# Attention and token mixer in one kernel: the attention-values product cut into 64x64 array tiles, its halves summed on VectorE

## The chip, the core and the metric

The kernel runs as one program on one core of a Trainium2 chip. The metric is the device time of one execution in microseconds (us). TensorE (PE in the profile) multiplies matrices into PSUM, which has eight banks; VectorE (DVE), ScalarE (ACT) and GpSimd (POOL) do the elementwise work; SyncE (SP) issues most of the DMA transfers. Every engine works through its own list in order.

## The reference

Causal softmax attention over 4 batches, 12 heads, 448 positions and 64 features per head, followed by a mixer over tokens and one over channels, all in float32 (x is the heads' outputs side by side, 4 x 448 x 768):

```python
scores = scale * np.matmul(q, k.transpose(0, 1, 3, 2))
scores = np.where(mask, -1000000000.0, scores)
...
attn = attn / (np.sum(attn, axis=-1, keepdims=True) + 1e-09)
attn_out = np.matmul(attn, v)
...
xt = x.transpose(0, 2, 1)
h = np.maximum(xt @ w_tok1, 0.0) @ w_tok2
u = x + h.transpose(0, 2, 1)
h2 = np.maximum(u @ w_ch1, 0.0) @ w_ch2
return u + h2
```

The causal mask means that of a head's 448x448 square only the lower triangle is computed.

## The kernel before

The work is cut into jobs. `plan.job(costs, fn, needs, holds, ...)` names the engines that may do a job, what it waits for and which buffers and PSUM banks it holds. Two tables of numbers in the code decide the rest: `PLACES` gives every job its place in one list (a smaller number goes first, if what it needs is ready by the costs that the jobs state), and `CHOICE` gives the engine (a, d, p, s for ScalarE, VectorE, GpSimd, SyncE) where several may do it. `Plan.emit` walks the list and writes the instructions of the five engines in that order. Where TensorE has nothing to do by these costs in the first 75 us of the program, `emit` writes a filler, a matmul on the mask tile whose result nobody reads (L865). A filler is an instruction like any other: it runs whether or not TensorE would have had to wait.

There are 24 pairs of heads (`g` from 0 to 23; the kernel's ranks are 2g). For each pair:

- `load_pair` and `load_rows` load Q, K and V. For pair 0 and from pair 6 on, Q and K come in blocks of 32x32 (L940, destinations kq, gh and gl), four transfers to a tensor, and VectorE turns them (`prep`, L988). For pairs 1 to 5 they come as rows (L892, L895) and TensorE turns them (L916, L910).
- `heads` makes the scores on TensorE in 64x64 tiles of the array (L1021), adds the mask and finds the maximum on VectorE (L1043), exponentiates on ScalarE (L1055), and takes the reciprocal of the sum on VectorE (L1077).
- `by_tensor` (pairs 0 to 9) divides and turns the probabilities on TensorE in 64x128 tiles (L1115); `by_dma` (pairs 10 to 23) turns them by DMA, with copies on VectorE and ScalarE (L640, L638). The result is the tile `pt`, with the key positions on the partitions.
- `values` multiplies V with `pt`. Its matmuls have 128 rows (keys) and 64 columns (a head's features), so two of them, one for each head, lie side by side in the array (L1245); two jobs `pv` per pair. The four ends of the triangle that are 64 keys wide, the tips, are a third job in 64x64 tiles (L1254). The left part of the 448 positions (192) goes to one PSUM bank (`low`), the right part (256) to another (`ps`). `evac` then copies the two parts to the tile `u` (helper `copy`: L632 on ScalarE, L634 on VectorE).
- After every second pair `xturn` turns `u` on TensorE in 64x128 tiles (L1291). Then follow `tokens` (L1350, L1383), and, batch by batch, the channel mixer (L1433; for the last two batches L1765, L1836, L1860). These have 128x128 tiles.

In the first 300 us the jobs of all these kinds are mixed on TensorE, so the shape of the tiles changes often. A matmul on float32 operands (L1021, L1245, L1254, L916) is two passes through the array, and shows as two records in the trace; one on fp32r, and a transpose, is one.

The two sets of pieces of the product are `PIECES` (pairs 0 to 9: eight pieces of 128 or 64 columns) and `SUMS` (pairs 10 to 23: four pieces of 256 or 128 columns).

Of the kernel before, what the change touches and what calls it, by code (L numbers as in the profile page):

```python
# [21 lines left out]
    "load_pair.blocks": {-2: (0, 1), 10: (129, 153), 12: (193, 224), 14: (242, 259), 16: (338, 293), 18: (405, 420),  # L22
        20: (522, 537), 22: (578, 591), 24: (670, 694), 26: (742, 758), 28: (831, 851), 30: (911, 927), 32: (996,
        1006), 34: (1056, 1070), 36: (1141, 1151), 38: (1205, 1220), 40: (1280, 1293), 42: (1333, 1348), 44: (1406,
        1426)},
    "load_pair.load": {0.5: (2,), 2.5: (3,), 4.5: (178,), 6.5: (209,), 8.5: (274,), 10.5: (312,), 12.5: (393,),
        14.5: (453,), 16.5: (490,), 18.5: (558,), 20.5: (615,), 22.5: (704,), 24.5: (773,), 26.5: (822,), 28.5:
        (902,), 30.5: (949,), 32.5: (1047,), 34.5: (1114,), 36.5: (1194,), 38.5: (1241,), 40.5: (1376,), 42.5:
        (1441,), 44.5: (1489,), 46.5: (1531,)},
    "load_pair.upper": {-0.2: (12,), 1.8: (15,), 3.8: (213,), 5.8: (245,), 7.8: (317,), 9.8: (380,), 11.8: (441,),  # L30
        13.8: (505,), 15.8: (519,), 17.8: (592,), 19.8: (651,), 21.8: (727,), 23.8: (821,), 25.8: (859,), 27.8:
        (938,), 29.8: (982,), 31.8: (1077,), 33.8: (1136,), 35.8: (1226,), 37.8: (1269,), 39.8: (1401,), 41.8:
        (1462,), 43.8: (1517,), 45.8: (1561,)},
# [500 lines left out]
def kernel(  # L534
# [74 lines left out]
    def act_ps(n):  # L609
        return 65.0 + 0.833 * n  # L610
# [1367 lines left out]
```

## Time and profile before

| | |
|---|---|
| median of 3 runs | 538.36 us (538.03 to 538.51) |
| the profiled execution | 538.04 us, of which the span from first to last instruction is 536.2 us |
| TensorE matmul busy | 529.8 us (99%) |
| VectorE, ScalarE, GpSimd busy | 426.4 (80%), 314.0 (59%), 164.2 us (31%) |
| granted TensorE clock | 1.00 over the span |

Busy times of matmuls overlap, since one starts while the one before still drains; how much time a matmul takes of the engine is read from the distance between two starts. The sums below are made against the profiled execution, 0.3 us under the median.

### The profile page before, as it was taken

The page shows a single profiled execution, that of the slowest core. Times are in us where ns is not written, and L with a number is a line of the kernel's source. Part 1 is how long each engine was busy: PE and PEld are TensorE (multiplying, and loading weights), DVE is VectorE, ACT ScalarE, POOL GpSimd, SP SyncE. Part 2 cuts the span into 40 slices and gives each one's busy share as a digit, 9 for nine tenths or more (in the row PEclk, how much of TensorE's full clock was granted, in tenths as well). Part 3 has the DMA queues.
Part 4 walks back from the last instruction along what each step waited for, and adds up shares of the span by engine and source line. Part 5 has one row for each costly group of instructions (what it writes and reads, how often), then busy time and mean ns, then how long its engine had stood idle before and what let it go on. Part 6 is the DMA issues. An engine that isn't in the chain of part 4 may idle for free.

```text
span 536.2 us, 12037 instructions
## 1 busy us (share of the span) xinstructions
PE 529.8 (99%) x4391; PEld 460.6 (86%) x4391; DVE 426.4 (80%) x1030; ACT 314.0 (59%) x768; POOL 164.2 (31%) x220
## 2 busy tenths in 40 slices
PE   8999999999999999999999999999999999999997
PEld 4778888888888888888898899999999999999996
DVE  5998899989797999888896679677877848485665
ACT  4998898899888787789784561243232313131300
POOL 2565745444252232332452132140010012321200
PEclk9999999999999999999999999999999999999999
DMA  9966677979999998999969327648213030212147
GB/s 194 198 116 144 152 214 160 215 153 233 207 178 200 225 190 193 205 196 229 210 163 198 115 92 205 131 119 162 88 32 116 7 91 23 87 32 88 31 75 131
DMA packets 221546, 77.72 MB, mean 145 GB/s; under 512 B 195760, under 2 KB 210992, under 8 KB 221488
## 3 DMA queue, kind: packets, MB, share of 16 engines
q1 hardware_dynamic: 207984, 74.90, 63.1%
q10 hardware_dynamic: 13504, 2.07, 2.1%
q8 instruction: 34, 0.56, 0.5%
q14 instruction: 24, 0.20, 0.2%
HBM read 49.15 MB, written 14.94 MB: 120 GB/s over the span
## 4 chain that ended last, share of the span: by engine, by line
PE 94%; SPq 2%; DVE 2%; ACT 1%; DMA 1%; issue 0%; POOL 0%; DVEq 0%; POOLq 0%
PE ps L1433 33%; PE ps L1860 16%; PE ps L1765 12%; PE ps L1021 6%; PE ps L1245 6%; PE ps L1383 6%; PE ps L1350 6%; PE ps L1836 3%; PE ps L1254 1%; PE ps L1115 1%; PE ps L1291 1%; SPq L940 1%; PE ps L865 1%; ACT prob L1055 1%; DMA gh<-in_k_dram 1%; PE ps L910 0%
## 5 line engine op out<-in xcount | busy, mean ns | idle before, releaser
L1500 DVE TENSOR_TENSOR u<-ps,u 128x448 f32<-128x448 f32 x118 | 72.5, 619 | 34.2 <-PE ps L1860 28.0
L1055 ACT ACTIVATE prob<-prob,stat 128x192 f32<-128x192 f32 (+6 forms) x168 | 83.7, 501 | 14.4 <-DVE stat L1043 14.1
L643 POOL TENSOR_TENSOR wl<-wf,wh 128x768 fp32r<-128x768 f32 x26 | 49.5, 1904 | 94.4 <-ACT wh L632 59.4
L1043 DVE CUSTOM_DVE_ANT_0 prob<-ps,mask 128x128 f32<-128x128 f32 (+6 forms) x168 | 63.3, 415 | 7.3 <-PE ps L1021 6.9
L634 POOL TENSOR_SCALAR prob<-prob,stat 128x64 f32<-128x64 f32 (+6 forms) x80 | 43.8, 559 | 55.4 <-DVE stat L1077 42.9
L1433 PE MATMUL ps<-uh,wh 128*128 128x448 f32 x144 | 53.7, 373 | 0.0
L1433 PE MATMUL ps<-gh,wh 128*128 128x448 f32 x144 | 52.9, 367 | 0.0
L1433 PE MATMUL ps<-gh,wl 128*128 128x448 f32 x144 | 52.7, 366 | 0.0
L1433 PE MATMUL ps<-gl,wh 128*128 128x448 f32 x144 | 52.7, 366 | 0.0
L1433 PE MATMUL ps<-uh,wl 128*128 128x448 f32 x144 | 52.7, 366 | 0.0
L1433 PE MATMUL ps<-ul,wh 128*128 128x448 f32 x144 | 52.7, 366 | 0.0
L632 ACT ACTIVATE wh<-wf 128x768 fp32r<-128x768 f32 x27 | 22.5, 846 | 51.2 <-PE ps L1860 25.8
L1021 PE MATMUL ps<-kq,kq 64*64 64x64 f32 (+5 forms) x768 | 45.4, 356 | 0.0
L1021 PEld LDWEIGHTS ps<-kq,kq 64*64 64x64 f32 x768 | 26.6, 133 | 15.5 <-issue 9.6
L1245 PE MATMUL ps<-pt,vraw 128*64 128x128 f32 (+2 forms) x544 | 37.3, 284 | 0.0
L1245 PEld LDWEIGHTS ps<-pt,vraw 128*64 128x64 f32 x544 | 28.2, 137 | 9.8 <-issue 2.1
L1795 DVE TENSOR_TENSOR kq<-kq,ps 128x448 f32<-128x448 f32 x35 | 21.2, 619 | 14.8 <-PE ps L1765 14.2
L1055 ACT ACTIVATION_READ_ACCUMULATOR prob<-prob,stat 128x1 f32 x168 | 32.1, 191 | 0.0
L638 ACT COPY pt<-pt 128x384 uint16<-128x384 uint16 (+3 forms) x41 | 31.6, 830 | 0.8 <-DMA pt<-prob 0.8
L1860 PE MATMUL ps<-u,wh 128*128 128x448 f32 (+1 forms) x110 | 31.0, 363 | 0.0
L1433 PEld LDWEIGHTS ps<-uh,wh 128*128 128x128 f32 x144 | 27.0, 188 | 2.8 <-issue 0.2
L1433 PEld LDWEIGHTS ps<-gl,wh 128*128 128x128 f32 x144 | 27.1, 188 | 2.5 <-DVE gl L1468 0.2
(222 smaller groups left out, 1403.2 us busy)
## 6 DMA issues: line engine op xcount, KB each, us to landing
wraw<-in_moe_w_ch_dram SPq DMA_DIRECT2D x24, 768.0 KB, 5.4
wf<-scratch SPq DMA_DIRECT2D x30, 384.0 KB, 3.1
scratch<-wf SPq DMA_DIRECT2D x24, 384.0 KB, 4.8
vraw<-in_v_dram SPq DMA_DIRECT2D x44, 96.0 KB, 3.4
kq<-in_k_dram SPq DMA_DIRECT2D x60, 56.0 KB, 3.7
kq<-in_q_dram SPq DMA_DIRECT2D x56, 56.0 KB, 2.4
out_dram<-h1l SPq DMA_DIRECT2D x24, 56.0 KB, 2.7
out_dram<-h1h SPq DMA_DIRECT2D x24, 56.0 KB, 2.2
```

The lines of the kernel that those rows point to most:

```text
L634: eng[e].tensor_scalar(dst, src, scale, 0.0, op0=ALU.mult, op1=ALU.add)
L643: eng[e].tensor_tensor(dst, a, b, op=ALU.subtract)
L1021: nc.tensor.matmul(scores[n].tile[lanes, to:at], lhsT=qe.tile[LANES[j], c * QC:(c + 1) * QC], rhs=ke.tile[LANES[j], slice(*keys)], start=T ...
L1043: nc.vector.tensor_tensor_reduce(out=part(c, r), in0=ps.tile[:, at:at + wide(c)], in1=mask[:, S - QC:S + P] if c == 2 else mask[:, S - wid ...
L1055: nc.scalar.activation(part(c, r), part(c, r), AF.Exp, bias=stat.tile[:, 0, AT[c]:AT[c] + 1], scale=-1.0, accum_out=stat.tile[:, 1, AT[c]: ...
L1245: nc.tensor.matmul(to, lhsT=s.tile[:, kb, j], rhs=rhs, start=(n in first_of), stop=False)
L1350: nc.tensor.matmul(ps.tile[:, :PART], lhsT=w[:, c, m * P:(m + 1) * P], rhs=x.tile[:, c, :], start=(n == 0), stop=(n == len(work) - 1),)
L1383: nc.tensor.matmul(ps.tile[:, :S], lhsT=h.tile[:, m, o * P:(o + 1) * P], rhs=w[:, m, :], start=(n == 0), stop=(n == 3 * NM - 1),)
L1433: nc.tensor.matmul(ps.tile[:, :S], lhsT=x.tile[:, at_:at_ + P], rhs=y, start=(n == 0 and i == 0), stop=(n + 1 == w[2] and i == 2),)
L1500: eng[e].tensor_tensor(u, ps.tile[:, :S], u, op=ALU.add)
L1765: nc.tensor.matmul(ps.tile[:, :S], lhsT=l()[:, t * P:(t + 1) * P], rhs=r, start=(t == 0 and n == 0), stop=(t == half - 1 and n == 2),)
L1860: nc.tensor.matmul(ps.tile[:, cols], lhsT=l.tile[:, t * P:(t + 1) * P], rhs=r.tile[:, cols], start=(n == 0), stop=(n == 3 * len(fs) - 1),)
```

## The change

The matmuls of the values product are split once more: the 128 keys of a piece become two halves of 64, so that each piece is four matmuls in 64x64 tiles instead of two in 128x64 tiles. The two halves can't be added in the array any longer: half 0 goes to the bank `ps`, half 1 to the bank `low`, each over all positions (half 0 has nothing in the first 64). The tips, which were 64x64 before, are written behind the second part in the same job. On the way out, `nought` copies all of `low` to `u` (ScalarE or VectorE), and `evac` adds 384 columns of `ps` on VectorE.

```diff
-        def chunks(n, j):
+        def chunks(n, j, half):
 
             if flat_:
-                which, kb, c, step, nq, o, stride = PIECES[n]
-                out = banks[which].tile[LANES[j]].rearrange("p (c q) -> p c q", q=QC)[:, c:c + step * (nq - 1) + 1:step]
-                rhs = pt.tile[:, 1 - j if c in OVER else j, o:o + stride * (nq - 1) + 1:stride]
+                _, kb, c, step, nq, o, stride = PIECES[n]
+                out = banks[half].tile[LANES[j]].rearrange("p (c q) -> p c q", q=QC)[:, c:c + step * (nq - 1) + 1:step]
+                rhs = pt.tile[LANES[half], 1 - j if c in OVER else j, o:o + stride * (nq - 1) + 1:stride]
...
                 for n in part:
+                    for half in range(2):
+                        for j in range(2):
+                            kb, to, rhs = chunks(n, j, half)
+                            nc.tensor.matmul(to, lhsT=s.tile[LANES[half], kb, j], rhs=rhs, start=n == 0, stop=False)
+                for half, kb, o, c in ENDS if part[0] else ():
                     for j in range(2):
-                        kb, to, rhs = chunks(n, j)
-                        nc.tensor.matmul(to, lhsT=s.tile[:, kb, j], rhs=rhs, start=(n in first_of), stop=False)
+                        nc.tensor.matmul(
+                            banks[half].tile[LANES[j], c * QC:(c + 1) * QC],
+                            lhsT=(ends if half else s).tile[LANES[half], kb, j], rhs=tip(o, c, j, half),
+                            start=False, stop=(o == 9),
+                        )
 
             prev = plan.job(
-                {"pe": 660.0 if part[0] else 718.0}, pv, js + pdone + [prev], [ps, low, s, ends, pt, u], rank, tiled=1
+                {"pe": 930.0 if part[0] else 705.0}, pv, js + pdone + [prev], [ps, low, s, ends, pt, u], rank, tiled=2
             )
...
-        prev = plan.job({"pe": 282.0}, tips, [prev], [ps, low, s, ends, pt, u], rank, tiled=2)
-
-        def evac(e):
+        def nought(e):
             if t == 0:
                 make(u, [P, NT, S], F32)
-            copy(e, u.tile[:, t, 3 * QC:], ps.tile[:, 3 * QC:S])
-            copy(e, u.tile[:, t, :3 * QC], low.tile[:, :3 * QC])
+            copy(e, u.tile[:, t], low.tile[:, :S])
+
+        def evac(e):
+            nc.vector.tensor_tensor(u.tile[:, t, QC:], ps.tile[:, QC:S], u.tile[:, t, QC:], op=ALU.add)
 
         first = [u_ready[b, 0]] if t else []
-        u_ready[b, t] = plan.job(
-            {"act": act_ps(S) + 65.0, "dve": dve1(S) + 70.0}, evac, [prev] + first, [ps, low, u], rank
-        )
+        c = plan.job({"act": act_ps(S), "dve": dve1(S)}, nought, [prev] + first, [low, u], rank)
+        u_ready[b, t] = plan.job({"dve": dve1(S - QC)}, evac, [prev, c], [ps, u], rank)
```

Both tables are new from end to end, so every engine's order changes, and which engine does what. A line of `CHOICE`:

```diff
-    "by_tensor.evac": {0: "dada", 2: "ddda", 4: "aaad", 6: "aada", 8: "adaa", 10: "aada", 12: "dada", 14: "ddaa",
+    "by_tensor.evac": {0: "daaa", 2: "dddd", 4: "adad", 6: "ddaa", 8: "aaaa", 10: "adda", 12: "daad", 14: "adaa",
```

Counted over TensorE's whole list, two neighbouring matmuls have tiles of different shape in 134 places before and in 120 after. Taking 128x128 as one group: it is left 37 times and entered 37 times before, 44 and 44 after; changes among the smaller shapes are 60 before and 32 after. Fillers are 27 before and 33 after, 16 and 13 of them ahead of the first scores. On VectorE the 24 adds are new, with five copies of 448 columns for two pairs of 192 and 256; ScalarE has 19 copies of 448 columns for 22 pairs of 192 and 256.

The first place is TensorE's list at the last values product (pair 23; matmuls of L1433, the channel mixer, stand ahead of it in both). Before:

```order
L1433 MATMUL ps_4606<-uh_2154,wl_4506 128x448
L1245 MATMUL ps_4648<-pt_4590,vraw_91 64x256 x2
L1245 MATMUL ps_4649<-pt_4590,vraw_91 64x128 x2
L1245 MATMUL ps_4648<-pt_4590,vraw_91 64x256 x2
L1245 MATMUL ps_4648<-pt_4590,vraw_91 64x128 x2
L1254 MATMUL ps_4648<-pt_4590,vraw_91 64x64 x2
L1254 MATMUL ps_4649<-pt_4590,vend_92 64x64 x2
L1254 MATMUL ps_4648<-pt_4590,vraw_91 64x64 x2
L1254 MATMUL ps_4649<-pt_4590,vend_92 64x64 x2
L1433 MATMUL ps_4672<-uh_1176,wh_4586 128x448
```

The same product after, from its second row on (L1246 are the pieces, L1249 the tips; ps_4829 is the bank of half 0, ps_4830 that of half 1):

```order
L1246 MATMUL ps_4830<-pt_4775,vraw_91 64x256 x2
L1246 MATMUL ps_4829<-pt_4775,vraw_91 64x128 x2
L1246 MATMUL ps_4830<-pt_4775,vraw_91 64x128 x2
L1246 MATMUL ps_4829<-pt_4775,vraw_91 64x256 x2
L1246 MATMUL ps_4830<-pt_4775,vraw_91 64x256 x2
L1246 MATMUL ps_4829<-pt_4775,vraw_91 64x128 x2
L1246 MATMUL ps_4830<-pt_4775,vraw_91 64x128 x2
L1249 MATMUL ps_4829<-pt_4775,vraw_91 64x64 x2
L1249 MATMUL ps_4830<-pt_4775,vend_92 64x64 x2
L1249 MATMUL ps_4829<-pt_4775,vraw_91 64x64 x2
L1249 MATMUL ps_4830<-pt_4775,vend_92 64x64 x2
L1348 MATMUL ps_4866<-xh_4792,w1hi 128x256
```

Eight rows of 128x64 tiles became sixteen matmuls of 64x64 tiles, of the same shape as the tips behind them; 22 matmuls of the token mixer (L1348) now stand between this product and the turn of `u` that waits for it, where six of the channel mixer stood.

The second place is the way out of the same product. Before, on ScalarE (u_3778 is the tile `u` of the last batch):

```order
L632 ACTIVATE prob_0_4657<-kq_4644 128x448
L632 ACTIVATE u_3778<-ps_4648 128x256
L632 ACTIVATE u_3778<-ps_4649 128x192
L632 ACTIVATE wh_4687<-wf_4642 128x768
L632 ACTIVATE xh_4717<-ps_4691 128x2x4x64
```

After, on VectorE (here both the copy and the add; in 19 pairs the copy is ScalarE's):

```order
L1466 SCALAR_TENSOR_TENSOR gl_4860<-ps_4794,gh_4841 128x448
L634 TENSOR_SCALAR u_3965<-ps_4830 128x448
L1265 TENSOR_TENSOR u_3965<-ps_4829,u_3965 128x384
L1361 SCALAR_TENSOR_TENSOR h1l_4897<-ps_4866,h1h_4895 128x256
L1361 SCALAR_TENSOR_TENSOR h1l_4897<-ps_4883,h1h_4895 128x256
```

Two copies on ScalarE became a copy and, behind it, an add on VectorE.

The third place is VectorE's list where it turns K of pair 8 (gh_786 before, gh_860 after; the load of that K is the fifth of the block loads L940 behind pair 0's on SyncE before and the sixth after). L1077 is a reciprocal that the division (L634) of the same probabilities waits for, L1363 (L1361 after) belongs to the token mixer. Before:

```order
L1077 RECIPROCAL stat_716<-stat_716 128x4
L988 STREAM_TRANSPOSE kq_915<-gh_786 128x448
L1363 SCALAR_TENSOR_TENSOR h1l_932<-ps_829,h1h_894 128x256
L634 TENSOR_SCALAR pt_939<-ps_900 128x448
L699 SCALAR_TENSOR_TENSOR wf_762<-wl_490,wf_762 128x224
L634 TENSOR_SCALAR prob_0_86<-prob_0_86,stat_716 128x320
```

After:

```order
L1265 TENSOR_TENSOR u_495<-ps_901,u_495 128x384
L988 STREAM_TRANSPOSE kq_1028<-gl_497 128x448
L1361 SCALAR_TENSOR_TENSOR h1l_1050<-ps_988,h1h_1024 128x256
L988 STREAM_TRANSPOSE kq_1056<-gh_860 128x448
L1361 SCALAR_TENSOR_TENSOR h1l_1050<-ps_1008,h1h_1024 128x256
L1077 RECIPROCAL stat_899<-stat_899 128x3
```

K of pair 8 moved ten rows back in VectorE's list (from row 138 to row 148), behind one add of the values product, and the division that stood four rows behind it no longer does. SyncE's list changes too: K of pair 1 as rows (uh, L892) is now the very first transfer, where it was the sixth row.

## Rows read from the trace of the kernel before

**Rows 1.** Page, span and busy time of each engine.

```profile
span 536.2 us, 12037 instructions
PE 529.8 (99%) x4391; PEld 460.6 (86%) x4391; DVE 426.4 (80%) x1030; ACT 314.0 (59%) x768; POOL 164.2 (31%) x220
```

**Rows 2.** Page, chain that ended last, by engine.

```profile
PE 94%; SPq 2%; DVE 2%; ACT 1%; DMA 1%; issue 0%; POOL 0%; DVEq 0%; POOLq 0%
```

**Rows 3.** Waits of PE over the span: total us, times, longest.

```profile
PE ps L865 <- POOL mask L650: 1.5, 1, 1.5
PE ps L916 <- DMA uh<-in_k_dram: 0.7, 1, 0.7
PE ps L1115 <- DVE stat L1043: 0.4, 1, 0.4
PE ps L1893 <- DVE u L1887: 0.3, 1, 0.3
```

**Rows 4.** Timeline of PE, last values product: start, length, instruction.

```profile
297.03 0.36 PE L1433 MATMUL ps<-ul,wh 128*128 128x448 f32 x1
297.23 0.36 PE L1433 MATMUL ps<-uh,wl 128*128 128x448 f32 x1
297.52 1.52 PE L1245 MATMUL ps<-pt,vraw 128*64 128x256 f32 x16
298.97 0.27 PE L1254 MATMUL ps<-pt,vraw 64*64 64x64 f32 x2
298.98 0.27 PE L1254 MATMUL ps<-pt,vend 64*64 64x64 f32 x2
299.08 0.22 PE L1254 MATMUL ps<-pt,vraw 64*64 64x64 f32 x2
...
299.13 0.23 PE L1254 MATMUL ps<-pt,vraw 64*64 64x64 f32 x2
...
299.19 0.23 PE L1254 MATMUL ps<-pt,vraw 64*64 64x64 f32 x2
...
299.36 0.48 PE L1433 MATMUL ps<-uh,wh 128*128 128x448 f32 x1
299.68 0.37 PE L1433 MATMUL ps<-ul,wh 128*128 128x448 f32 x1
```

**Rows 5.** Windows of L1021, four 64x64 scores of 256 or 320 columns start.

```profile
151.06:151.28 0.22, 0.21 (x4) 0.16 (x8) 1.00 0.60 104
151.28:151.49 0.21, 0.21 (x8) 0.13 (x1) 1.00 0.80 126
```

**Rows 6.** Timeline of PE, first 47 us, fillers and waits.

```profile
8.44 0.99 PE L916 MATMUL ps<-ident,ul 112*64 112x112 f32 x16
9.36 0.82 PE L865 MATMUL ps<-mask 128*128 128x512 bf16 x3
10.87 0.99 PE L916 MATMUL ps<-ident,uh 112*64 112x112 f32 x16 [0.68 <-DMA uh<-in_k_dram]
...
17.48 0.38 PE L865 MATMUL ps<-mask 128*128 128x512 bf16 x1
...
45.15 0.27 PE L1115 MATMUL ps<-ident,prob 64*128 64x64 f32 x1
45.83 0.65 PE L1115 MATMUL ps<-ident,prob 64*128 64x64 f32 x13 [0.41 <-DVE stat L1043]
```

**Rows 7.** Timeline of DVE, 40 to 45 us.

```profile
41.34 0.18 DVE L1077 RECIPROCAL stat<-stat 128x4 f32<-128x4 f32 x1
42.70 0.65 DVE L988 STREAM_TRANSPOSE kq<-gh 128x448 f32<-128x448 f32 x1 [1.18 <-DMA gh<-in_k_dram]
```

**Rows 8.** Timeline of SP, 30 to 43 us.

```profile
33.86 1.55 SPq L953 DMA_DIRECT2D vraw<-in_v_dram  x1
35.45 2.15 SPq L940 DMA_DIRECT2D gl<-in_q_dram  x4
37.65 2.04 SPq L940 DMA_DIRECT2D gh<-in_k_dram  x4
```

**Rows 9.** Windows, all engines, 50 to 300 us: PE, PEld, DVE, ACT, POOL.

```profile
50.00:300.00 250.00, 250.00 (x2486) 213.10 (x2486) 219.50 (x604) 207.87 (x528) 97.81 (x128) 1.00 0.91 192
```

**Rows 10.** Groups by form, VectorE, ScalarE and fillers: busy us, mean ns.

```profile
L1043 DVE CUSTOM_DVE_ANT_0 prob<-ps,mask 128x384 f32<-128x384 f32 x24 | 13.1, 547 | 0.0
L634 DVE TENSOR_SCALAR pt<-ps 128x448 f32<-128x448 f32 x16 | 9.7, 614 | 0.4 <-PE ps L1115 0.3
L632 ACT ACTIVATE pt<-ps 128x448 f32<-128x448 f32 x24 | 12.5, 533 | 0.0
L632 ACT ACTIVATE u<-ps 128x256 f32<-128x256 f32 x22 | 8.3, 378 | 12.6 <-PE ps L1254 12.4
L632 ACT ACTIVATE u<-ps 128x192 f32<-128x192 f32 x22 | 7.1, 324 | 0.0
L865 PE MATMUL ps<-mask 128*128 128x512 bf16 x27 | 8.7, 449 | 1.5 <-POOL mask L650 1.5
```

**Rows 11.** Timeline of PE, a product's tips to the turn of u.

```profile
150.78 0.27 PE L1254 MATMUL ps<-pt,vraw 64*64 64x64 f32 x2
...
151.01 0.22 PE L1254 MATMUL ps<-pt,vraw 64*64 64x64 f32 x2
...
151.98 0.71 PE L1291 MATMUL ps<-ident,u 64*128 64x64 f32 x16
```

More of the change, by code (lines that the diff above doesn't have):

```diff
@@ new lines @@
+    "channels.down": {28.5: (699,), 28.75: (735,), 29: (743,), 29.25: (761,), 29.5: (806,), 29.75: (781,), 36:
[6 rows of a table added]
+    "add.plus": {-6: (718, 756, 758, 775, 820, 790, 1090, 1073, 1080, 1055, 1127, 1121, 1180, 1153, 1214, 1221,
[6 rows of a table added]
+    "store.turn": {-5: (1752, 1768, 1785, 1786, 1798, 1807, 1843, 1837, 1861, 1856, 1876, 1870, 2236, 2237, 2242,
+        2243, 2245, 2251, 2253, 2257, 2262, 2266)},
+    "store.send": {-5: (1754, 1772, 1787, 1794, 1801, 1809, 1847, 1840, 1864, 1858, 1878, 1873, 2238, 2241, 2247,
+        2246, 2252, 2254, 2261, 2258, 2265, 2267)},
@@ new lines @@
+    "combined.sum_.do": {-4.94: (1886, 1888, 1889, 1892), -4.93: (1957, 1960, 1964, 1967), -4.92: (2018, 2019, 2022,
+        2024), -4.91: (2086, 2088, 2089, 2096), -4.9: (2143, 2146, 2151, 2156)},
+    "group.product.do": {55.44: (1880,), 55.71: (1885,), 55.98: (1908,), 56.25: (1905,), 56.52: (1932,), 56.79:
[5 rows of a table added]
+    "group.first.do": {-6: (1887, 1950, 2021, 2084, 2159)},
+    "group.plus.do": {-6: (1913, 1918, 1920, 1938, 1939, 1931, 1940, 1995, 1996, 1999, 2002, 2005, 2006, 2009, 2059,
+        2061, 2067, 2069, 2073, 2072, 2076, 2129, 2131, 2130, 2142, 2144, 2140, 2148, 2198, 2203, 2199, 2204, 2207,
+        2225, 2211)},
@@ L1226, in chunks @@
             view = pt.tile.rearrange("p o (j q) -> p o j q", j=2)
-            return kb, banks[c == 1].tile[LANES[j], c * QC:(c + nq) * QC], view[:, o, 1 - j if c in MIXED else j]
+            out = banks[half].tile[LANES[j], c * QC:(c + nq) * QC]
+            return kb, out, view[LANES[half], o, 1 - j if c in MIXED else j]
         def tip(o, c, j, half):
@@ L1249, in values @@
             )
-        def tips(e):
-            for half, kb, o, c in ENDS:
-                for j in range(2):
-                    nc.tensor.matmul(
-                        banks[half].tile[LANES[j], c * QC:(c + 1) * QC],
-                        lhsT=(ends if half else s).tile[LANES[half], kb, j], rhs=tip(o, c, j, half),
-                        start=False, stop=(o == 9),
-                    )
-        prev = plan.job({"pe": 282.0}, tips, [prev], [ps, low, s, ends, pt, u], rank, tiled=2)
```

297 lines of the change are left out of this document (139 added, 158 removed), and 198 rows, old and new, of tables (CHOICE, PLACES).

## The prediction

> **What bounds the kernel now.** I read the busy shares first: matmuls cover 529.8 us of a span of 536.2 [rows 1], and the chain that ended last lies on TensorE for 94% [rows 2]. Busy alone proves little, since matmuls overlap. So I looked at TensorE's waits: four places, 2.9 us in all [rows 3], of which 1.5 us is the start of the program. Between 50 and 300 us TensorE has no idle time at all, while VectorE is busy 219.5 and ScalarE 207.9 us of the 250 [rows 9]. The kernel is therefore as long as TensorE's list plus small waits in the first 50 us, and only what shortens the list, or those waits, shortens the kernel. VectorE, with 30.5 us free of 250, is the next engine that could bind.
>
> What TensorE's list costs beyond its columns is seen in one values product [rows 4]. The channel matmuls of 448 columns start 0.20 us apart. From the last of them to the first 128x64 matmul it is 0.29, so leaving the 128x128 shape costs 0.09. The tips' rounds start 0.06 us apart, but the first of them lasts 0.11, so the first round in a new shape costs 0.05. From the product's first start to the tips' it is 1.45 us. The product is 1536 columns of rounds (256, 256, 128, 128 twice, two passes included): 24 steps of 64 columns, at the tips' 0.055 a step 1.32 us. The rest, 0.13, is the first round's 0.05 and a drain of 0.08 before the tips' shape. On the way back, the last round to the first channel matmul takes 0.17 for 0.06, and that matmul 0.32 for 0.20. So a change of shape costs 0.14 us on leaving 128x128, 0.23 on coming back, and 0.13 among the small shapes (0.15 if the 256-column rounds are a little quicker per column than the tips').
>
> **The change, part by part.**
>
> Columns: nothing. The product has the same rounds after as before; only each holds four 64x64 tiles in place of two of 128x64. Would four run beside each other? The tips do it before: in the steps of 0.055 us four matmuls of 64 columns start, two to each bank, in the layout that the pieces have after [rows 4]. And four scores of 256 and 320 columns start together, with no other start for 0.22 us [rows 5], which is four steps of 0.055. So I cost the columns at zero; the bound is one of the rivals.
>
> TensorE: Matmul & The Clock Gate in the Trainium skill (section "Wait — 56ns, not 53.3ns?") says that two matmul starts never come closer than about 25 ns, however small they are. By that rule a round of four would take at least 100 ns, and the 64-column rounds would lose 42 ns each. Rows 4 speak against it: four starts fit into 55 ns here, so the rows' figure stands.
>
> Changes of shape: before 37 x 0.14 + 37 x 0.23 + 60 x 0.13 = 21.5 us, after 44 x 0.14 + 44 x 0.23 + 32 x 0.13 = 20.4, a gain of 1.1; with 0.15 among the small shapes 22.7 and 21.1, a gain of 1.6. The gain is small because only half of it is the new shape's doing: the product no longer has a change inside, but the new list leaves 128x128 seven times more often. I take 1.5, near the upper value, because the long rounds of rows 5 (0.22 for 256 columns while two of the four have 320) say that a wide column is not dearer than a tip's.
>
> Fillers: 33 for 27. One takes (0.82 - 0.38) / 2 = 0.22 us [rows 6], so six more cost 1.3 us if TensorE would otherwise have had work, and nothing if it would have waited in their place. I take the full 1.3.
>
> Waits of the start. TensorE loses 0.68 us at 10.87 us, behind three fillers, for K of pair 1 [rows 6]. That transfer now goes first of all, and its turn stands ahead of the first scores; I take the wait as gone. At 45.15 us a transpose starts and the next comes 0.68 us later, where 0.06 is usual, so 0.62 us is lost [rows 6]. The row names VectorE, and on VectorE the 1.18 us of idleness is at the turn of K of pair 8, waiting for its load [rows 7]; the load was issued at 37.65 us because the V transfer ahead of it held SyncE's list for 1.55 us [rows 8]. After the change the load stands one block load later on SyncE, but the turn ten rows later on VectorE, and the division that TensorE waited for no longer stands behind it. I take this wait as gone as well: together 1.3 us. If both stay, nothing.
>
> VectorE: 24 adds of 384 columns at 0.55 us, by the nearest row of that width from PSUM, make 13.1 us [rows 10]. Five copies at 0.61 [rows 10] in place of two pairs, each of as many columns and so at least 0.61, add 1.8 at most. That makes 14.9 us, against 30.5 free between 50 and 300 us [rows 9]; the list also moves other work off VectorE, whose list grows from 1017 to 1035 rows although 24 adds came. ScalarE loses 22 x (0.38 + 0.32) = 15.4 us and gains 19 x 0.53 = 10.1 [rows 10]. Both lie beside TensorE's work and I cost them at nothing. What hides them is the work that TensorE has between a product and the next turn of `u`. If that cover is gone the price is the longer way out: copy and add are 0.53 + 0.55 = 1.08 us where two copies were 0.70, so 0.38 us at each of the 12 turns.
>
> The sum: -1.5 + 1.3 - 1.3 = -1.5 us. Against the profiled execution of 538.04 that is 536.5; the median of the runs lies 0.3 above it, so **536.8 us**, 0.3% faster. A difference of 0.2% (1.1 us) is about what a measurement of this kernel can tell from no change.
>
> **The rivals.**
>
> 1. The start gives the gain back. The new list puts nine more fillers behind the first scores and three fewer ahead; if these stand in holes that the loads really make, TensorE's other waits may also stay: -1.5 + 1.3 = -0.2, to a wait of the same size as today's more, +0.3 or so. Time 538.2 (537.3 to 538.9), no change that can be told. For it: the fillers are put where the list itself sees nothing ready. Against: both waits of today have a named cause, which the list moves.
>
> 2. VectorE comes late, and the kernel is slower. Place: the turn of `u`, which waits for the add. Before, 0.97 us lies between the last round of tips and the turn [rows 11], and the copies took 0.70 of it. If the turn still came as close, TensorE would wait 0.38 us and, where the add stands behind other work on VectorE (busy 88% there [rows 9]), one of its instructions of 0.6 us more: 12 x 0.98 = 11.8 us, less 1.5, so up to 548.7. It decides the sign at an average of (1.5 + 1.1) / 12 = 0.22 us a turn. Against it: in the list shown, 22 matmuls stand between where six stood. The skill's TensorEngine Tiling (Array Packing), section "PSUM Bottleneck", warns of this side of the change: faster tiles leave the way out of PSUM as the bottleneck, and both ScalarE and VectorE should share it; here the add can only be VectorE's.
>
> 3. A matmul has a floor of its own that four small tiles hit: 64-column rounds take twice as long, 0.055 us more, in 80 rounds (ten products of pairs 0 to 9 with four such pieces, two passes each), 4.4 us: 541.2. The floor of the Trainium skill (TensorE: Matmul & The Clock Gate, named above) would make it 3.4. Only rows 4 speak against both, and clearly.
>
> 4. The change doesn't do what it says: the two key halves run one after the other. Then 24 x 1.32 us come on top, some 568. Rows 4 and 5 are nearly proof against it.
>
> 5. More is gained than I sum: fillers that only stand where TensorE would wait cost nothing, and all waits go: -1.6 - 1.3 = -2.9, 535.4 and below.
>
> **How the numbers follow.** Chances: the forecast (535.4 to 537.3) 0.55, rival 1 0.27, rival 2 0.07, rival 3 0.03, rival 4 0.01, rival 5 below the range 0.07. Faster by over 0.2% (under 537.3): 0.55 + 0.07 = 0.62. Within 0.2%: 0.27. Slower: 0.11. The range goes from rival 5's edge, 535.4, to 538.7, which is the sum with no wait removed and half a microsecond for new ones; it leaves out rivals 2 to 4 and the part of rival 5 below, 0.18. The likeliest case alone has 535.4 to 537.3.
>
> **What the new profile would show.** Right: no 128x64 matmuls; rounds of four, 0.055 us per 64 columns, in the pieces as in the tips; no step of 0.1 us ahead of the tips; TensorE's waits for uh and for stat gone; no wait of the turns of `u` (L1289) on VectorE. The channel part behind 320 us, which the change only shifts, starts about 1.5 us earlier. Wrong: waits of L1289 or L1115 on VectorE between 50 and 300 us (rival 2); steps of over 0.06 us in the tips or 64-column pieces (rival 3); or new waits in the first 70 us beside the fillers (rival 1).

## The result: 0.6% slower, and the profile after

The changed kernel takes 541.99 us (median of 7 runs, 541.0 to 542.44) where the kernel before takes 538.03 (7 runs on the same chip): ratio 1.0063, 95% interval 1.0046 to 1.0079. The forecast was 536.8 with 535.4 to 538.7, so sign and size are both wrong. The profiled execution took 542.44 us.

The page after, span and busy times, and the engines of the chain that ended last:

```profile
span 540.5 us, 13133 instructions
PE 530.8 (98%) x4941; PEld 462.2 (86%) x4941; DVE 427.3 (79%) x1051; ACT 318.7 (59%) x750; POOL 167.2 (31%) x217
...
PE 78%; DMA 10%; DVE 5%; SPq 4%; issue 1%; ACT 1%; ACTq 0%; DVEq 0%
```

Against [rows 1, 2] no engine is much busier, but only 78% of the chain is TensorE where it was 94%, and DMA has gone from 1% to 10%: the chain that ended last now runs through transfers, which VectorE or TensorE waited for. Its waits after (engine, line, releaser, total us, times, longest):

```profile
PE ps L865 <- POOL mask L650: 1.5, 1, 1.5
PE ps L1431 <- DVE wl L643: 0.9, 1, 0.9
PE ps L1021 <- DVE kq L988: 0.8, 1, 0.8
PE ps L1348 <- DVE gl L1466: 0.8, 1, 0.8
PE ps L1246 <- DVE pt L634: 0.5, 1, 0.5
PE ps L916 <- DMA ul<-in_q_dram: 0.5, 1, 0.5
PE ps L910 <- DMA uh<-in_k_dram: 0.5, 1, 0.5
PE ps L1891 <- DVE u L1885: 0.3, 1, 0.3
PE ps L916 <- DMA uh<-in_k_dram: 0.2, 1, 0.2
```

In [rows 3] the waits between the first filler and the finish were 1.1 us; here they are 4.2. The two that the forecast called gone are nearly gone (uh 0.7 to 0.2, L1115 behind stat 0.4 to nothing worth a row), and six others have come.

Where along the program? The last stage begins with the group products, which stand on the path in both kernels. The rows of the line of the group products, one operand (duration in ns min/median/max, then first and last start), of the kernel before and of the changed one:

```profile
L1765 PE MATMUL ps<-uh,u x30: 362/365/369, 372.2 to 479.1; 128*128 128x448 f32 x30
```

```profile
L1763 PE MATMUL ps<-uh,u x30: 368/368/368, 375.1 to 483.0; 128*128 128x448 f32 x30
```

The first of them starts 2.9 us later, as much as the 3.1 us of new waits (4.2 - 1.1) less the 0.2 that the forecast gave without its term for waits (-1.5 + 1.3). From the first to the last of them it takes 107.9 us for 106.9: another 1.0 us is lost where nobody waits. Matmuls of 448 columns start 205.3 ns apart there, for 203.4 before (the steps are taken up at the run of the kernel before). The remaining 0.4 of the 4.3 us between the two spans comes behind them.

One of the new waits, followed back. TensorE after, around 140 us (start, length, instruction, wait):

```profile
139.31 1.49 PE L1246 MATMUL ps<-pt,vraw 64*64 64x256 f32 x32
...
142.65 0.39 PE L1348 MATMUL ps<-xh,w1hi 128*128 128x256 f32 x1 [0.82 <-DVE gl L1466]
```

VectorE there:

```profile
139.64 0.65 DVE L988 STREAM_TRANSPOSE kq<-kq 128x448 f32<-128x448 f32 x1 [2.41 <-DMA kq<-in_q_dram]
140.21 0.52 DVE L695 TENSOR_SCALAR wf<-wf 128x768 int32<-128x768 int32 x1
140.65 0.55 DVE L640 COPY prob<-prob 128x768 uint16<-128x768 uint16 x1
141.11 0.95 DVE L699 SCALAR_TENSOR_TENSOR wf<-wraw,wf 128x768 int32<-128x768 int32 x1
141.98 0.62 DVE L1466 SCALAR_TENSOR_TENSOR gl<-ps,gh 128x448 fp32r<-128x448 f32 x1
```

A turn of Q waits 2.41 us for its transfer. Behind it in VectorE's list stand three long instructions and then the one that frees the bank which TensorE needs. The wait of L1431 at 277 us is built alike: a merge of pt (L640) waits 1.86 us for a DMA, and L643 stands three rows behind it.

The product itself did what it was to do. An early product shows it: from its pieces at 27.97 us to its tips at 29.36 it takes 1.39 us, where a product of the same pieces took 1.49 before (27.34 to 28.83 us of the first trace). The step ahead of the tips is gone, and tips start 0.05 to 0.06 apart:

```profile
27.97 1.57 PE L1246 MATMUL ps<-pt,vraw 64*64 64x128 f32 x64
29.36 0.23 PE L1249 MATMUL ps<-pt,vraw 64*64 64x64 f32 x2
...
29.41 0.23 PE L1249 MATMUL ps<-pt,vraw 64*64 64x64 f32 x2
```

Those 1.39 us hold 16 rounds of four (64 records), 8 of them of 64 columns like the tips': 24 steps, 0.056 us each behind the first round's 0.05. So rivals 3 and 4 are out. The Trainium skill (TensorE: Matmul & The Clock Gate, section "Wait — 56ns, not 53.3ns?") has at least about 25 ns between two starts, which would make 0.1 us of four, an estimate from that figure; here four fit into 0.06.

### The profile page after: what moved, and what is told of

It is laid out like the page before. It is cut to its first block, busy times and chain, and to the rows that moved or that the text cites. A ratio compares the mean times of both kernels' runs of the same rounds, so it can differ in the third digit from the quotient of the medians.

```text
span 540.5 us, 13133 instructions
## 1 busy us (share of the span) xinstructions
PE 530.8 (98%) x4941; PEld 462.2 (86%) x4941; DVE 427.3 (79%) x1051; ACT 318.7 (59%) x750; POOL 167.2 (31%) x217
## 4 chain that ended last, share of the span: by engine, by line
PE 78%; DMA 10%; DVE 5%; SPq 4%; issue 1%; ACT 1%; ACTq 0%; DVEq 0%
PE ps L1431 28%; PE ps L1858 14%; PE ps L1763 12%; PE ps L1021 5%; PE ps L1348 5%; PE ps L1246 5%; PE ps L1381 4%; DMA pt<-prob 3%; PE ps L1834 3%; DMA out_dram<-kq 3%; SPq L940 2%; DMA kq<-in_q_dram 2%; PE ps L1115 1%; PE ps L1289 1%; DVE prob L1043 1%
## 5 line engine op out<-in xcount | busy, mean ns | idle before, releaser
L1055 ACT ACTIVATE prob<-prob,stat 128x448 f32<-128x448 f32 (+6 forms) x168 | 83.9, 501 | 13.5 <-DVE stat L1043 13.0
L643 POOL TENSOR_TENSOR wl<-wf,wh 128x768 fp32r<-128x768 f32 x25 | 46.8, 1873 | 69.6 <-ACT wh L632 67.2
L1043 DVE CUSTOM_DVE_ANT_0 prob<-ps,mask 128x256 f32<-128x256 f32 (+6 forms) x168 | 63.9, 415 | 4.6 <-PE ps L1021 3.7
L634 POOL TENSOR_SCALAR prob<-prob,stat 128x384 f32<-128x384 f32 (+6 forms) x85 | 48.0, 575 | 50.7 <-DVE stat L1077 43.7
L1431 PE MATMUL ps<-uh,wh 128*128 128x448 f32 x144 | 54.0, 375 | 0.0
L1431 PE MATMUL ps<-gh,wl 128*128 128x448 f32 x144 | 52.7, 366 | 0.9 <-DVE wl L643 0.9
L1431 PE MATMUL ps<-gh,wh 128*128 128x448 f32 x144 | 53.3, 370 | 0.0
L1431 PE MATMUL ps<-gl,wh 128*128 128x448 f32 x144 | 52.7, 366 | 0.0
L1431 PE MATMUL ps<-ul,wh 128*128 128x448 f32 x144 | 52.6, 365 | 0.0
L1431 PE MATMUL ps<-uh,wl 128*128 128x448 f32 x144 | 52.4, 364 | 0.0
L1021 PE MATMUL ps<-kq,kq 64*64 64x64 f32 (+5 forms) x768 | 46.5, 358 | 0.8 <-DVE kq L988 0.8
L1021 PEld LDWEIGHTS ps<-kq,kq 64*64 64x64 f32 x768 | 27.3, 133 | 19.2 <-issue 9.9
L1246 PE MATMUL ps<-pt,vraw 64*64 64x128 f32 (+2 forms) x1088 | 39.4, 279 | 0.6 <-DVE pt L634 0.5
L1246 PEld LDWEIGHTS ps<-pt,vraw 64*64 64x64 f32 x1088 | 33.1, 133 | 7.2 <-issue 1.3
L638 ACT COPY prob<-prob 128x1024 uint16<-128x1024 uint16 (+1 forms) x37 | 34.1, 942 | 4.0 <-DVE prob L634 1.9
L638 ACT COPY pt<-pt 128x512 uint16<-128x512 uint16 (+3 forms) x37 | 29.8, 864 | 2.9 <-DMA pt<-prob 2.8
L988 DVE STREAM_TRANSPOSE kq<-kq 128x448 f32<-128x448 f32 x30 | 18.9, 637 | 15.0 <-DMA kq<-in_k_dram 11.9
L1431 PEld LDWEIGHTS ps<-gh,wl 128*128 128x128 f32 x144 | 27.1, 188 | 3.5 <-DVE wl L643 1.3
```

Source lines behind the costliest of these rows:

```text
L634: eng[e].tensor_scalar(dst, src, scale, 0.0, op0=ALU.mult, op1=ALU.add)
L638: nc.scalar.copy(out, in_)
L643: eng[e].tensor_tensor(dst, a, b, op=ALU.subtract)
L1021: nc.tensor.matmul(scores[n].tile[lanes, to:at], lhsT=qe.tile[LANES[j], c * QC:(c + 1) * QC], rhs=ke.tile[LANES[j], slice(*keys)], start=T ...
L1043: nc.vector.tensor_tensor_reduce(out=part(c, r), in0=ps.tile[:, at:at + wide(c)], in1=mask[:, S - QC:S + P] if c == 2 else mask[:, S - wid ...
L1055: nc.scalar.activation(part(c, r), part(c, r), AF.Exp, bias=stat.tile[:, 0, AT[c]:AT[c] + 1], scale=-1.0, accum_out=stat.tile[:, 1, AT[c]: ...
```

## The experiments

Theory A: the new product saves what the forecast says, and the new tables cost the time. Theory B: the adds make VectorE late for TensorE. Theory C: the fillers are work in full. A fourth, that TensorE was never the only bound ahead of 150 us, came from the first runs. Each ratio is to the kernel before in the same set of runs (medians 538.13, 537.83, 537.74 and 538.66 in the four sets, each on a chip of its own); the bracket behind it is its 95% interval.

**The changed kernel again** (no edit).

> The changed kernel once more, unchanged, to see whether its waits are a matter of its list or of one execution. If the list makes them (theory A: the new list lets VectorE wait for late transfers with work behind it that TensorE needs), TensorE waits again at about 58 us for pt, at 141 us behind L1466 and at 277 us behind L643, together 2.2 us by the profile's waits within 0.5. If they are chance, they stand elsewhere. Time 541 to 542.5 either way.

543.07 us (6 runs, 541.26 to 545.23), 1.0081 (1.0051 to 1.0112), a little above what was expected. The waits behind L643 (1.3 us) and L1466 (0.5) are there again, that of L1246 on pt L634 is not; two others at turns of u came, behind the add and behind its copy (L1289: 1.1 and 0.7). The list makes some of its waits; others come and go from one execution to the next.

**Old tables, new product.** In the kernel before, the loops of the pieces are those of the change; tips and way out keep their places in the old lists:

```diff
-            copy(e, u.tile[:, t, 3 * QC:], ps.tile[:, 3 * QC:S])
-            copy(e, u.tile[:, t, :3 * QC], low.tile[:, :3 * QC])
+            copy(e, u.tile[:, t], low.tile[:, :S])
+            nc.vector.tensor_tensor(u.tile[:, t, QC:], ps.tile[:, QC:S], u.tile[:, t, QC:], op=ALU.add)
```

> The kernel before with its own two tables; only the product's matmuls are cut into 64x64 tiles, and the copies give way to a copy and an add at the same place in the lists. TensorE's changes of shape fall from 134 to 110, all 24 among the small shapes: 24 x 0.13 = 3.1 us less. Theory A (the new tables cost the time, the new product saves): 535.0, between 534.3 and 536. Theory B (the 24 adds make VectorE late for TensorE): 538 or above, with over 2 us of TensorE's waits on VectorE behind 50 us. A floor or lack of overlap of the four tiles: 541 or above without such waits.

544.2 us (540.9 to 545.63), 1.0092 (1.0058 to 1.0126), not the 535.0 of theory A. TensorE's waits in its trace, the first two rows that are not of the start:

```profile
PE ps L1293 <- DVE u L1268: 3.7, 3, 1.5
...
PE ps L1115 <- DVE u L1268: 1.0, 2, 0.6
```

L1293 is the turn of u, L1268 the add. This is rival 2 at its place, in the old tables. In the new tables the turns meet it less: no row in the first trace, 1.8 us in the second.

**New tables, old product** (4 runs). In the changed kernel the matmuls are the old ones, `nought` makes the two old copies, and the add is left out:

```diff
-            nc.vector.tensor_tensor(u.tile[:, t, QC:], ps.tile[:, QC:S], u.tile[:, t, QC:], op=ALU.add)
+            pass
```

> The changed kernel's tables with the old product: 128x64 tiles, two copies on the engine that has the copy, no add; the add's job is empty. TensorE has 168 changes of shape, 48 small ones more than the changed kernel: 48 x 0.13 = 6.2 us. Theory A: the waits stay, 542 + 6.2 = about 548. Theory B: with 24 adds gone from VectorE the waits of 2.5 to 4 us go too, 544 to 545.5.

545.74 us (545.66 to 545.83), 1.0131 (1.0099 to 1.0163), next to B's 544 to 545.5. TensorE's list is 6.2 us longer than the changed kernel's, the time by the ratios only 2.7 us (to the 1.0081 of this set) or 3.7 (to 1.0063). The waits at 141 and 277 us are gone from its trace.

**No late fillers**: the changed kernel writes only its first 13 fillers.

```diff
-                        self.filler.fn(e)
+                        self.fillers = getattr(self, "fillers", 0) + 1
+                        if self.fillers <= 13:
+                            self.filler.fn(e)
```

> The changed kernel without the 20 fillers behind the first scores. Theory C (fillers are work in full, 0.22 us each): 4.4 us less, some 537.5, and the start of the program no longer gives anything away. If they stand where TensorE would wait in any case: 541 to 542, waits in their place. If TensorE's granted clock falls in the first 75 us without them: slower than 543.

543.36 us (541.79 to 544.36), 1.0085 (1.0055 to 1.0116), beside 543.07 with them. Theory C falls: the 20 fillers stand where TensorE would wait in any case. The granted clock was 1.00 over the first 75 us without them too.

**The kernel before again** (no edit).

> The kernel before once more, for a trace from the chip of these experiments. 537 to 539; its 128x128 matmuls of 448 columns behind 380 us start about 203.4 ns apart, as in the first trace, if the 205 of the four kernels with the new tables is a matter of the list, and 205 if it is a matter of the chip.

537.37 us. Its 448-column matmuls between 380 and 520 us start 203.4 ns apart (mean of some 680 steps of 190 to 212 ns), as in the first trace (203.4) and in all traces with the old tables (203.4 to 203.5); with the new tables throughout 204.8 to 205.4. It is the list, not the chip.

**New tables, old tail.** `PLACES` and `CHOICE` of the jobs of the last stage come from before (the edit in short):

```diff
+for n in PLACES: if n.split(".")[0] in ("store", "mixtures", "reread", "group", "hidden", "combined", "spared", "finish"): both tables of before
```

> The changed kernel with the kernel before's places and engines for the jobs of the last stage alone (mixtures, combined tiles, group products, group up and down, stores, finish). In the four traces with new tables the 448-column matmuls behind 380 us are about 2 ns further apart, which is about 1.3 us in all. If the order of the tail makes that, 1.3 us less than the changed kernel, 540.5 to 541.5, with 203.4 ns behind 450 us, where TensorE's list is that of before. If not, no change.

542.61 us (541.76 to 544.89), 1.0089 (1.0068 to 1.0109): not to be told from the changed kernel's. The steps fell to 203.8 ns (204.1 behind 450 us, where 203.4 was expected), so the order of the last stage sets most of the difference, some 680 x 1.6 ns = 1.1 us. That this shortens the kernel is not shown: the mixed list brought a wait of its own, 0.7 us for GpSimd's pt.

**Old tables, new product, no adds**: as the second run, without its added line, so half of the product's sum is missing.

> The old tables with the new product, without the 24 adds: half of the product's sum is left out. TensorE's list and the order of everything else are those of the run with the adds (544.2). If the adds on VectorE are what makes TensorE wait there (theory B): no waits of the turns of u on VectorE, 538.1 - 24 x 0.13 = 535.0, between 534 and 536. If four tiles cost TensorE more by themselves, or the clock falls by them without any wait: 541 or above.

537.97 us (12 runs, 535.55 to 539.49), 1.0001 (0.9987 to 1.0016). The adds account for the whole loss in these tables (4.9 us by the ratios, 6.2 by the medians). But the 3.1 us that the shorter list should give are not there either. TensorE's waits in its trace, an execution of 539.19 us:

```profile
PE ps L1256 <- issue: 1.8, 1, 1.8
...
PE ps L1115 <- DVE stat L1043: 1.2, 1, 1.2
PE ps L1292 <- ACT u L632: 0.8, 1, 0.8
PE ps L916 <- DMA uh<-in_k_dram: 0.8, 1, 0.8
```

That is 4.6 us in four places, where the trace of before on the same chip has 1.2 us in all beside start and finish (0.7 of it where the first trace has fillers). Behind 152 us the saving does come through; the section on why the prediction was wrong has the rows.

**Only the first pair of each turn** has the new product (`cut = t % NTH == 0`), in the old tables; 12 adds instead of 24.

> The old tables; the new product only in the first of the two pairs of each turn of u, the old one in the second, which the turn waits for most closely. 12 shape changes and 12 adds in place of 24. By theory B the price of an add is paid where a turn stands close behind it: 538.1 - 12 x 0.13 = 536.5, between 535.8 and 537.5, faster than both kernels. If an add costs wherever it stands: 539 to 541.

539.78 us (12 runs), 1.0032 (1.0019 to 1.0046): slower than before, as for "an add costs wherever it stands". In its trace (538.25 us, among its fastest) the turns don't wait for these adds; a transpose of L1115 waits 0.4 us for one.

**New tables, no adds**: the changed kernel with `pass` in place of its add; half of the sum is missing.

> The changed kernel without its 24 adds (half of the product's sum is left out); TensorE's list and everything else as in the changed kernel (542.6 to 543 here). In the old tables the 24 adds were worth 544.2 - 538.0 = 6.2 us. If VectorE has no more room in the new tables than in the old ones, 537 here; if the new tables made room for half of it, 539 to 540; if the adds cost nothing in the new tables and its start and order cost all: 542 to 543.

541.52 us (540.3 to 543.66), 1.0062 (1.0040 to 1.0083). Against the 1.0063 and 1.0081 of the changed kernel the adds are worth 0.1 to 1.0 us in the new tables, which can't be told from nothing: the new tables have room for them that the old ones lack. What is left, 1.0062 against 1.0001 for the same product without adds in the old tables, is 3.3 us of the new tables by themselves (1.9 to 4.7 by the two intervals).

**The kernel before with more adds**: the old product, and behind its two copies one more add of 256 columns, so that its right part is added twice.

```diff
+            nc.vector.tensor_tensor(u.tile[:, t, 3 * QC:], ps.tile[:, 3 * QC:S], u.tile[:, t, 3 * QC:], op=ALU.add)
```

> The kernel before, product and tables untouched, with one more add of 256 columns behind the two copies of each pair, always on VectorE (it adds the right part of the product a second time, so the output is another one). This is the price of VectorE's time alone, without four small tiles or a longer list of TensorE. 24 adds of 0.42 us are 10 us for 13.1 of the change. If the adds alone made the 6.2 us, 538 + 6.2 x 10 / 13.1 = 542.7, 541.5 to 544. If they cost only together with the new product: 538 to 539.

539.45 us (12 runs), 1.0029 (1.0017 to 1.0042): 1.7 us for 10 us of VectorE's time. So VectorE's time is not free, but it is not worth its length either, and scaled to 13.1 us it makes 2.2, less than half of what the adds cost beside the new product.

**Old tables, new product, VectorE relieved**: divisions of the pairs 10 to 23 that VectorE has go to GpSimd.

```diff
-                    copy(e, part(c, r), part(c, r), stat.tile[:, 2, AT[c]:AT[c] + 1])
+                    copy("pool" if e == "dve" else e, part(c, r), part(c, r), stat.tile[:, 2, AT[c]:AT[c] + 1])
```

> The old tables with the new product and its adds (544.2), and with VectorE relieved: the 27 divisions of probabilities that VectorE has in pairs 10 to 23 are given to GpSimd at the same place, some 10 us. If VectorE's time is what binds, most of what the adds cost in those 14 pairs comes back, 544.2 - 6.2 x 14 / 24 = 540.6, 539.5 to 541.5. If it is the place of the add ahead of the turns and not VectorE's time: 543 to 545. If GpSimd, slower, comes late in its place: above 545.

541.46 us (540.65 to 542.99), 1.0066 (1.0047 to 1.0085). It looks like the expected recovery, but the turns still wait 2.6 us for the add and L1115 1.0. What is gone is the longest wait (1.5 to 1.1) and what came behind it, a fall of the clock (last section): the two runs with all adds whose mean clock was at least 0.999 took 540.9 and 542.03. Whether relief gives anything beyond that stays open.

**No adds once more**, for its trace.

> The old tables, the new product, no adds, once more for its trace. In the first trace TensorE stood still for 2.0 us at 81.3 us inside the tips, waiting for nothing that the profile shows, while 16 KB of its instructions were being fetched; the fetch had started 267 instructions late. If the late fetch of a longer list makes that, this trace has a fetch over 150 instructions late between 60 and 100 us again, with or without a standstill; if the standstill was chance of another kind, no fetch is over 110 late.

537.55 us, a packet of instructions some 230 late at 73.0 us, and no standstill there. Its waits on stat (1.4), u (0.7), ul (0.6) and prob (0.7) make 3.4 us.

**Less work for TensorE, early and late**: the kernel before without 24 matmuls of the low half of u (`a, b = 0, 24` and `200, 224`); a small correction term is missing in some blocks.

```diff
                 for i, (x, y) in enumerate(((w[0], hi), (w[0], lo), (w[1], hi))):
+                    skipped[0] += i == 1
+                    if i == 1 and a < skipped[0] <= b:
+                        continue
```

> The kernel before, tables and product untouched, without the first 24 of the channel mixer's matmuls of the low half of u (ul,wh; a small correction term is left out of a few blocks). They lie between about 65 and 120 us; each is 203 ns of TensorE, 4.9 us in all, and no other engine loses work. If TensorE alone is the bound there, as the prediction had it, 537.8 - 4.9 = 532.9 (532.5 to 533.5). If VectorE and the others follow so closely there that what TensorE saves turns into waits, 535 to 537.5.

> The same 24 matmuls less, but the 201st to 224th of them, at about 300 to 320 us, where VectorE is busy 70% and less. Both theories: TensorE alone is the bound there, 532.9 (532.5 to 533.5).

Early: 537.83 us (12 runs), 0.9987 (0.9971 to 1.0003). Late: 534.8 us (6 runs), 0.9928 (0.9910 to 0.9946). The same 4.9 us are worth about 0.7 at 65 to 120 us (none to 1.6 by the interval) and 3.9 at 300 us (2.9 to 4.8). Both times lie above the expected ranges; the kernel before was 0.9 us above the 537.8 that these took. The early one's trace shows the saving come and go, set beside the second trace of before matmul by matmul. The same matmuls, at about 65, 109 and 152 us, of before:

```profile
65.13 0.47 PE L1433 MATMUL ps<-uh,wh 128*128 128x448 f32 x1
...
108.75 0.37 PE L1433 MATMUL ps<-gh,wl 128*128 128x448 f32 x1
...
151.86 0.47 PE L1433 MATMUL ps<-uh,wh 128*128 128x448 f32 x1
```

and with 24 matmuls less ahead of 109 us:

```profile
65.77 0.47 PE L1438 MATMUL ps<-uh,wh 128*128 128x448 f32 x1
...
105.66 0.36 PE L1438 MATMUL ps<-gh,wl 128*128 128x448 f32 x1
...
151.64 0.47 PE L1438 MATMUL ps<-uh,wh 128*128 128x448 f32 x1
```

TensorE starts 0.6 us late, is 3.1 us ahead at 109 us and 0.2 at 152. Its waits in that stretch with a row of their own:

```profile
PE ps L1245 <- DVE pt L640: 0.5, 1, 0.5
PE ps L1291 <- ACT u L632: 0.3, 1, 0.3
PE ps L1115 <- DVE h1l L1363: 0.3, 1, 0.3
```

The rest goes in steps too short for a row: at the product at 109 us, behind h1l of VectorE at 121 us, at the turns of u at 125 and 151 us. The late one keeps 4.3 us of its 4.9 in its trace.

**Two moves in VectorE's list of the changed kernel**: the turn of Q at 139.6 us behind L1466, the merge of pt at 276.1 us behind L643.

```diff
+        for name, nth, behind, at in (("prep.turn", 21, "channels.lo", 3), ("merged.merge", 28, "parts.<lambda>", 1)):
```

> The changed kernel complete, with two instructions of VectorE moved in its list: the turn of Q (L988) at 139.6 us stands behind L1466 instead of four rows ahead of it, the merge of pt (L640) at 276.1 us behind L643 instead of three rows ahead. These two wait for transfers in all traces of the new tables with the new product, and TensorE waits 0.5 to 1.3 us behind each. If that is so, 1.5 us less than the changed kernel (541.99 and 543.07 in its two sets): 540.5 to 541.5. If TensorE then only waits elsewhere: 542 to 543.

541.88 us (11 runs, 539.27 to 544.67), 1.0064 (1.0045 to 1.0083), against 1.0063 and 1.0081 unmoved: no gain that can be told, where 1.5 us was expected. Both waits are gone from the trace, and TensorE waits elsewhere (1.0 us on stat, 0.6 on pt).

**New product in six late pairs** (12, 14 to 22) of the old tables.

> The old tables, the new product only in pairs 12, 14, 16, 18, 20 and 22: the first pair of each turn, behind 100 us, where the traces of the runs with the old tables gained most (150 to 300 us of the program). Six shape changes less, 0.8 us, and six adds of 0.55 us on VectorE. If the gain comes through there: 537.8 - 0.8 = 537.0 (536.5 to 537.5), faster than both kernels; if adds cost wherever they stand, by the 12 of the run with the first pairs (+1.9): 538 to 539.

538.13 us (12 runs), 0.9995 (0.9979 to 1.0012): nothing to be told. In its trace each of these products behind 136 us gains some 0.1 us, and one wait of 0.8 us for pt (L638) at 266 us gives it back. No version with the new product beats the kernel before.

## Why the prediction was wrong

**The step that failed** is the end of its first part: "only what shortens the list, or those waits, shortens the kernel". It was drawn from a TensorE without idle time between 50 and 300 us and a VectorE with 30.5 us free in those 250. Ahead of 150 us that does not hold: 24 matmuls less there, 4.9 us, gave 0.7, and at 300 us 3.9. A list of TensorE without gaps says that nothing is late; it does not say that TensorE alone is the bound. The means of 250 us hid the others. The same windows in slices of 25 us, kernel before, second trace (PE, PEld, DVE, ACT, POOL):

```profile
25.00:50.00 25.00, 24.50 (x439) 19.81 (x437) 24.07 (x93) 24.43 (x85) 17.72 (x42) 1.00 0.70 141
50.00:75.00 25.00, 25.00 (x385) 20.79 (x383) 23.41 (x75) 23.47 (x73) 15.53 (x21) 1.00 0.62 153
75.00:100.00 25.00, 25.00 (x385) 21.34 (x385) 22.35 (x63) 20.96 (x60) 11.31 (x20) 1.00 0.94 189
100.00:125.00 25.00, 25.00 (x219) 21.25 (x221) 23.14 (x61) 24.02 (x59) 10.89 (x16) 1.00 0.87 183
...
175.00:200.00 25.00, 25.00 (x239) 21.11 (x238) 22.89 (x67) 20.47 (x53) 7.94 (x12) 1.00 1.02 190
```

Of the four slices from 25 to 125 us three have VectorE 93 to 96% and ScalarE 94 to 98% busy beside a full TensorE; the fourth (89 and 84%) and those behind 125 us have less (from 175 to 200 us 92 and 82%).

**Changes of shape, -1.5.** Four tiles run beside each other and the step ahead of the tips is gone, as costed. The term is a difference: by its prices the new product alone takes 24 small changes away, 3.1 us, and the new tables bring 2.1 us back, seven more departures from 128x128 and returns for four small changes less. What the 3.1 are worth depends on the place. From the turn of u at 152 us to the first channel matmul behind the last product, kernel before, second trace:

```profile
151.86 0.47 PE L1433 MATMUL ps<-uh,wh 128*128 128x448 f32 x1
298.59 0.48 PE L1433 MATMUL ps<-uh,wh 128*128 128x448 f32 x1
```

and old tables, new product, no adds, second trace:

```profile
153.62 0.47 PE L1434 MATMUL ps<-uh,wh 128*128 128x448 f32 x1
298.88 0.47 PE L1434 MATMUL ps<-uh,wh 128*128 128x448 f32 x1
```

That is 146.7 us and 145.3 (145.1 in the first trace without adds): the ten products between save 1.5 us, at least the 10 x 0.13 of the price. Ahead of 152 us the other fourteen save nothing: TensorE is 1.8 us late there, 3.6 in the first trace, behind waits that the kernel before did not have. So the price held where TensorE alone is the bound, and the place decided.

**Fillers, +1.3.** As work they cost nothing: 20 fewer left the time where it was, with waits in their place. The term was on the wrong side of the bounds that the text gave ("nothing if it would have waited in their place"). Whether the new tables leave TensorE more such holes, 20 fillers behind the first scores for 11, is what rival 1 says, and no run tells it.

**Waits of the start, -1.3.** Their causes were rightly named and are nearly gone; in their place TensorE waits for K of pair 0 (L988, 0.8), Q of pair 1 (0.5) and K for L910 (0.5). Rival 1 had this, but not the waits behind 50 us. All new waits together are 3.1 us, where the term had 1.3 less.

**VectorE and ScalarE at nothing.** Wrong, with the price depending on the tables: the adds are worth 5 to 6 us in the old ones (with the clock's fall in four of six runs), 0.1 to 1.0 in the new ones, and other adds 1.7 us beside the old product. Rival 2 had the engine but not the whole of the place: it looked at the turns of u (L1289), which wait in the changed kernel's second trace, and in its first VectorE is late for L1348, L1431 and L1246. For L1348 and L1431 it had itself waited for a transfer. Such a wait was looked for behind the add alone, not behind every transfer that VectorE's list meets.

**What the sum left out**: the new tables themselves cost 3.3 us without any add. By the traces that is mostly list and not waits. TensorE's waits beside start and finish are alike without adds, 4.4 us in the new tables, 5.4 and 4.2 in the two traces of the old; the spans less these are 535.4 against 532.0 and 531.6 us. An estimate, which no run tests: 2.1 us are the changes of shape that the new tables add, by the prediction's prices, and 1.1 the pitch of the last stage (its order sets it; by what means is open). So 2.1 of the 3.3 stood in the forecast, hidden in its difference. In the old tables about half of the product's saving came through; in the new ones the tables cost more than that.

In rival 3 the second figure should be 3.6 us, (100 - 55) ns in 80 rounds; it decides nothing.

## What to carry to other kernels

Before you sum up the list of the engine that never waits, find out place by place what a saving is worth: leave out a few of its instructions there and measure. Look at the other engines in slices as short as the stages; where they are as full as the first, expect savings to come back as waits. The shares alone do not settle it: VectorE was 89 to 92% busy from 175 to 250 us too, where the saving came through. Work that is added to a full engine costs by what stands behind it in order, and a wait for a transfer anywhere in that engine's list counts as well. Where a table of places is refitted along with a change, run the change in the old table and the old code in the new one, and put their shares into the sum apart: here a saving of 3.1 us by price and a table of 3.3 us stood behind one small difference.

## What the runs showed of the hardware

**The clock can fall behind one long wait.** In the run with the old tables and the new product, TensorE:

```profile
240.82 0.27 PE L1293 MATMUL ps<-ident,u 64*128 64x64 f32 x1
242.58 0.71 PE L1293 MATMUL ps<-ident,u 64*128 64x64 f32 x15 [1.49 <-DVE u L1268]
243.22 0.56 PE L1435 MATMUL ps<-uh,wh 128*128 128x448 f32 x1
243.57 0.58 PE L1435 MATMUL ps<-ul,wh 128*128 128x448 f32 x1
```

and the windows of one us there (the granted clock is the third column from the right):

```profile
241.00:242.00 1.00, 0.09 (x1) 0.00 (x0) 0.03 (x1) 0.94 (x2) 0.86 (x2) 1.00 1.17 213
...
244.00:245.00 1.00, 1.00 (x4) 0.92 (x3) 1.00 (x9) 1.00 (x5) 0.00 (x0) 0.50 0.90 179
245.00:246.00 1.00, 1.00 (x4) 0.88 (x4) 1.00 (x6) 1.00 (x5) 0.50 (x2) 0.50 1.30 196
246.00:247.00 1.00, 1.00 (x5) 0.90 (x4) 1.00 (x4) 1.00 (x4) 0.14 (x1) 0.56 1.92 18
```

TensorE stands still for 1.49 us, does small transposes, and then runs at 1.2 GHz (granted 0.50) for some 3.4 us: matmuls of 448 columns are 0.35 to 0.38 us apart, not 0.20. That adds some 1.7 us to the wait. The wait alone does not decide it. At an earlier turn of u in the same trace it was as long, and the granted clock stayed at 1.00:

```profile
156.17 0.71 PE L1293 MATMUL ps<-ident,u 64*128 64x64 f32 x16 [1.51 <-DVE u L1268]
```

What else it takes is not shown. Four of the six runs, the traced one among them, had a mean clock of 0.995 and took 543.9 to 545.6 us, the other two 540.9 and 542.0.

**A standstill beside a late packet of instructions.** In the first run without adds TensorE stopped inside the tips for 1.81 us with nothing to wait for:

```profile
81.20 0.28 PE L1256 MATMUL ps<-pt,vraw 64*64 64x64 f32 x4
...
83.29 0.27 PE L1256 MATMUL ps<-pt,vend 64*64 64x64 f32 x2 [1.81 <-issue]
```

The page after counts 39 packets of instructions on one queue, that of before 34, 16 KB each. With 4941 matmuls and as many weight loads that is 253 instructions to a packet; 64x64 tiles double those of the product. In that trace a packet starts at 81.05 us and is 0.96 us under way. Counted against an even spacing of 256, from the packet that came earliest in its trace, it starts some 270 instructions late. In the ten traces with the new product throughout, the latest packet between 60 and 100 us is some 160 to 270 late, in the six with the old product at most some 120. A standstill of 0.9 us or more without a named cause came with two of the latest, this one and one of 0.9 us in the scores of the run with the first pairs (some 240 late). Three packets of 220 to 230 late had none, and this one had landed 1.3 us before TensorE went on. That the late packet makes the standstill, and that the transfers around it delay the packet (many small blocks of Q are loaded there), is likely and not shown.
